# Holding back the output stores of six steps and issuing them from GpSimd in steps 6 and 7 of an mLSTM and mixture-of-depths kernel

## The chip, the core and the metric

The kernel runs on one core of a Trainium2 chip. The core has a matrix engine (TensorE, PE in the profile), a vector engine (DVE), a scalar engine (ACT), GpSimd (POOL) and SyncE (SP), which here only issues DMAs, and 16 DMA engines that all queues share. The engines run side by side and wait for each other through semaphores; each takes its own instructions strictly in order. The metric is the device time of one execution in microseconds, the median of several runs.

## What is computed

The reference has two parts. The first is an mLSTM cell over 4 batches, 8 heads, 768 time steps and a head size of 40, with a matrix state C and a normalizer n for each head:

```python
m_new  = np.maximum(f_gate[:, :, t] + m, i_gate[:, :, t])
f_stab = np.exp(f_gate[:, :, t] + m - m_new)
i_stab = np.exp(i_gate[:, :, t] - m_new)
C = f_stab * C + i_stab * outer(v[t], k[t])
n = f_stab * n + i_stab * k[t]
y[t] = sigmoid(o_gate[t]) * (C @ q[t]) / maximum(abs(n @ q[t]), 1.0)
```

The second is a mixture of depths over the rows x (4 x 768 rows of 320): each batch ranks its rows by a score, and the best 128 go through an MLP and are added back.

```python
scores = x @ w_gate
out = x.copy()
top = argpartition(-scores[b], 128)[:128]
ye  = maximum(x[b, top] @ w1, 0) @ w2
out[b, top] = x[b, top] + sigmoid(scores[b, top]) * ye
```

## The kernel before

The recurrence is worked in blocks of 256 time steps: 3 blocks for each of 4 batches make 12 steps, numbered n = 0 to 11, with batch n // 3. A step is some 8 us long and is a fixed list of work that `_fast` writes out by hand for all engines (the loop of lines 675 to 743); no planner reorders it. For the core of a step TensorE makes `scores(n)`, the transposes of the next step's k and q (`turn`), the state update of the next step (`update`), the reading of the states (`read`), and `attend(n)`; DVE masks, adds up states, and divides (`divide`, which gives y, line 346); ACT copies the transposes out of PSUM and makes the sigmoids.

GpSimd's part matters here. In each step it has `weigh(n + 2)` (line 244: v times the gate columns, two instructions, which wait for the load of v), `output(n)` (line 354: y times the sigmoid gives the rows `x`) and `store(n)` (line 361: two DMAs of 160 KB that write the 256 rows of the step to `out` in DRAM). The rows lie in `x_t`, two buffers that batches use in turn, so steps 0 to 2 write the first, 3 to 5 the second, and 6 to 8 the first again.

Loads of k, v, q, the output gate and the MLP's weights are all issued by SyncE from a queue written by hand (`queue`, line 624), with up to eight in flight; a load waits until its buffer is free, and there are four buffers each for k, v and q.

The second part runs between steps. When a batch's three steps are done its rows are ranked (`ranks`), the 128 chosen row numbers are made (`numbers`, `index`), and GpSimd gathers the chosen rows from `out` in DRAM into `xe` with an indirect DMA (`fetch`, line 523). So a gather reads what the batch's stores wrote. `fetched` then transposes `xe` on TensorE (line 533), `layer1` and `layer2` are the MLP, and `add` scatters its result into `out` with an indirect DMA that adds in DRAM. For batch 0 the row numbers are made in step 4 and fetch(0) is issued in step 6; batch 1 is ranked, gathered and, with batch 0, taken through the MLP in step 8, which has a list of its own (`layers`, lines 628 to 673) that begins, behind the step's scores, with `fetched(0)`. In this list the outputs and stores of steps 6, 7 and 8 stand as well, behind fetch(1). Batches 2 and 3 follow in steps 9 to 11 and at the end.

Some idle places of TensorE hold matmuls that compute nothing (`fill`, line 221).

Of the kernel before, what the change touches and what calls it, by code (L numbers as in the profile page):

```python
# [26 lines left out]
def _fast(ctx, tc, q, k, v, i_gate, f_gate, o_gate, w_gate, w1_in, w2_in, out):  # L27
# [186 lines left out]
    def widen(n):  # L214

        ACT.copy(out=qw_t[n % 2][:, :, :, 0:D], in_=q_t[n % NB].rearrange("s h (t d) -> s t h d", t=2))  # L216
# [30 lines left out]
    def sigmoid(n):  # L247
        for r in range(2):
            for c in range(2):
                ACT.activation(out=so_t[n % 3][64 * c:64 * c + 64, r], in_=o_t[n % NO][64 * r:64 * r + 64, c], func=AF.Sigmoid)  # L250
# [8 lines left out]
    def update(n):  # L259


        spare(n)
        pU = pending[n]["pUt"][:, :, 0:2 * NP * D1].rearrange("e c (p r x) -> e c p r x", r=2, x=D1)
        for c in range(2):
            for p in range(NP):
                for j in range(2):
                    PE.matmul(pU[64 * j:64 * j + 64, c, p], k_t[n % NB][:, c, 2 * p + j, :], wv_t[n % 3][:, c, 2 * p + j],  # L267
                              start=True, stop=True)
        pending[n]["pU"] = pU

    def states(n, i0=0, i1=4):

        for i in range(i0, i1):
            if n % NS == NS - 1 and i == 3:
                return
            C = work.tile([128, NP, D1], FP, name="C", bufs=12)
            src = pending[n]["pU"][:, i // 2, :, i % 2]
            if (n, i) in state:
                DVE.tensor_tensor(out=C, in0=src, in1=state[n, i], op=OP.add)  # L279
                src = C  # L280
            if i < 3:
                if src is not C:
                    DVE.tensor_copy(out=C, in_=src)
                state[n, i + 1] = C
            else:
                b, s = divmod(n + 1, NS)
                DVE.tensor_tensor(out=C, in0=src, op=OP.mult, in1=cols[s][:, 4, b * NP:b * NP + NP].unsqueeze(2)
                                  .to_broadcast([128, NP, D1]))
                state[n + 1, 0] = C

    def scores(n):
        kT, qT = pending[n]["kT"], pending[n]["qT"]
        pS = ps_s.tile([128, 2, 2, NP, 64], FP, name="pS", tag="s")
        for c in range(2):
            for p in range(NP):
                for j in range(2):
                    for r in range(2):
                        e, o = slice(64 * j, 64 * j + D), slice(64 * r, 64 * r + 64)
                        t = slice(128 * c + 64 * r, 128 * c + 64 * r + 64)
                        PE.matmul(pS[o, j, c, p, :], kT[e, p, t], qT[e, p, t], start=True, stop=True)  # L300
        pending[n]["pS"] = pS

    def masked(n):
        P = work.tile([128, 2, 2, NP, 64], FP, name="P")
        flat = "s j c p t -> s (j c p) t"
        DVE.tensor_tensor(out=P.rearrange(flat), in0=pending[n].pop("pS").rearrange(flat), op=OP.mult,  # L306
                          in1=mask.unsqueeze(1).to_broadcast([128, 4 * NP, 64]))
        pending[n]["P"] = P
# [48 lines left out]
    def store(n):  # L357
        b, s = divmod(n, NS)
        for c in range(2):
            a = 256 * s + 128 * c  # L360
            (POOL if n < N - 1 else SP).dma_start(out=out[b, a:a + 128, :].rearrange("(r t) d -> t r d", t=64),  # L361
                          in_=x_t[b % 2][64 * c:64 * c + 64, 2 * s:2 * s + 2, 0:DM])

    def router(n):
        b, s = divmod(n, NS)
        x = x_t[b % 2][:, 2 * s:2 * s + 2]
        scr = work.tile([128, DM], FP, name="scr", bufs=1)
        for r in range(2):
            DVE.tensor_tensor_reduce(out=scr, in0=x[:, r, 0:DM], in1=wg, scale=1.0, scalar=0.0,  # L369
                                     op0=OP.mult, op1=OP.add, accum_out=x[:, r, DM:DM + 1])  # L370
        del pending[n]
# [53 lines left out]
    def ranks(b):  # L425
        x, d = x_t[b % 2], dep[b]
        d["cnt"] = mod.tile([128, 2 * NS], FP, name="cnt")
        for r in range(2 * NS):
            (greater if r < NS else signs)(b, d["sb"], x[:, r, DM:DM + 1], d["cnt"][:, r:r + 1])
        halved(d)  # L430
# [39 lines left out]
    def select(b):  # L470
        sel = mod.tile([128, 2 * NS, 128], BF, name="sel", bufs=1)
        DVE.tensor_tensor(out=sel, in0=iota.unsqueeze(1).to_broadcast([128, 2 * NS, 128]),
                          in1=dep[b]["cnt"].unsqueeze(2).to_broadcast([128, 2 * NS, 128]), op=OP.is_equal)
        dep[b]["sel"] = sel
# [45 lines left out]
    def fetch(b):  # L520

        d = dep[b]
        POOL.indirect_dma_start(out=xe_t[b % 2][:, 0:DM], out_offset=None, in_=out[0:b + 1].rearrange("b s d -> (b s) d"),  # L523
                                in_offset=bass.IndirectOffsetOnAxis(ap=d["idx"], axis=0),
                                bounds_check=(b + 1) * S - 1, oob_is_err=False)
# [102 lines left out]
    def layers(n):  # L628

        fetched(0)  # L630
        read(n)
        ranks(1)
        select(1)
        attend(n)
        layer1(0, 0)
        numbers(1, ps_t.tile([128, 3], FP, name="pi", tag="t"))
        fetch(1)
        sigmoid(n - 2)
        output(n - 2)
        store(n - 2)  # L640
        layer1(0, 4)
        divide(n)
        valued(0)
        sigmoid(n - 1)
        output(n - 1)
        store(n - 1)
        layer2(0)
        router(n - 2)
        router(n - 1)
        fetched(1)  # L650
        weighed(0)
        sigmoid(n)
        output(n)
        store(n)
        valued(1)
        layer1(1, 0)
        router(n)
        layer1(1, 4)
        weigh(n + 1)
        add(0)  # L660
        turn(n + 1, "kT")
        widen(n + 1)
        pB = spread(2, 0, 2 * NS, ps_h, False)
        turn(n + 1, "qT")
        dep[2] = {"sb": spread_copy(pB, 2 * NS)}
        ranks(2)
        layer2(1)
        weighed(1)
        select(2)
        weigh(n + 2)  # L670
        update(n + 1)
        states(n + 1)
        add(1)

    for n in range(N):
        b, s = divmod(n, NS)
        more = n + 1 < N
        todo = queue.get(n, ())
        for act, i in zip(todo[0::2], todo[1::2]):
            act(*(() if i is None else (i,)))  # L680
        scores(n)
        masked(n)
        if n == 8:
            layers(n)
            continue
        if n == 0:
            update(0)
            states(0)
        if n in (3, 6, 11):
            router(n - 1)  # L690
        if n == 4:
            ranks(0)
            select(0)
        if more:
            turn(n + 1, "kT", (0, 2, 6, 2, 2, 4)[n] if n < 6 else 0)
            widen(n + 1)
        if 0 < n and more:
            update(n + 1)
            if n != 9:
                states(n + 1)  # L700
            if n not in (3, 6, 7, 9):
                router(n - 1)
        if not more:
            sigmoid(n)
            gated(n)
            fill(ps_t.tile([128, 128], FP, name="pf", tag="t"), 2)
        read(n)
        if n == 9:
            numbers(2, ps_s.tile([128, 2, 512], FP, name="pi", tag="s")[:, 0, 0:3])
            states(n + 1)  # L710
        if n + 2 < N and n != 7:
            weigh(n + 2)
        if n == 6:
            fetch(0)
        if n == 0:
            update(1)
            states(1)
        if more:
            turn(n + 1, "qT")
            if n in (3, 7):  # L720
                dep[n // 4] = {"sb": spread(n // 4, 0, 2 * NS)}
            if n not in (6, 7):
                sigmoid(n)
        else:
            fetched(b - 1, 2)
            dep[b] = {"sb4": spread(b, 0, 4)}
            layer1(b - 1, 0)
            valued(b - 1)
            ranks_first(b)
        attend(n)  # L730
        divide(n)
        if n == 4:
            numbers(0, spare(n + 1)[:, 1, 0:3])
        if n == 9:
            fetch(2)
        if more and n not in (6, 7):
            output(n)
            store(n)
        if n == 0:
            POOL.memset(k_t[3][:, :, :, D:DP], 0.0)  # L740
            tables()
        if n == 1:
            margins()
# [376 lines left out]
```

## Time and profile before

| | us |
|---|---|
| median of 3 runs | 163.75 (161.92 to 165.38) |
| the profiled execution, its own time | 163.37 |
| its span, first to last instruction | 161.3 |
| granted TensorE clock, mean over the span | 0.989 of full speed |
| GpSimd's DMA queue: bytes, share of the 16 engines' span | 4.92 MB, 11.0% |
| SyncE's DMA queue: bytes, share | 18.75 MB, 65.1% |

The profile is one execution taken by the hardware profiler. A row in order of time gives the start, the busy time, the engine, the line, the operation, output and inputs with their shapes, and how many instructions were merged; the bracket at its end is the idle time of that engine just before, and what released it. A matrix product of float32 appears as two or more instructions. In the rows of DMA issues stand the number of DMAs, the size of each and the median time from the issue to the landing; in those of a queue the packets, the megabytes and the share of all 16 engines in the stretch asked for. A row for a stretch of time gives the busy time of each engine with its count of instructions, then the granted clock, the DMA share (packets in flight overlap, so that it can exceed 1) and GB/s. [...]

### The profile page before, as it was taken

The page shows a single profiled execution, that of the slowest core. Times are in us where ns is not written, and L with a number is a line of the kernel's source. Part 1 is how long each engine was busy: PE and PEld are TensorE (multiplying, and loading weights), DVE is VectorE, ACT ScalarE, POOL GpSimd, SP SyncE. Part 2 cuts the span into 40 slices and gives each one's busy share as a digit, 9 for nine tenths or more (in the row PEclk, how much of TensorE's full clock was granted, in tenths as well). Part 3 has the DMA queues.
Part 4 walks back from the last instruction along what each step waited for, and adds up shares of the span by engine and source line. Part 5 has one row for each costly group of instructions (what it writes and reads, how often), then busy time and mean ns, then how long its engine had stood idle before and what let it go on. Part 6 is the DMA issues. An engine that isn't in the chain of part 4 may idle for free.

```text
span 161.3 us, 6676 instructions
## 1 busy us (share of the span) xinstructions
PE 144.5 (90%) x2864; PEld 125.4 (78%) x2864; DVE 95.2 (59%) x251; ACT 89.0 (55%) x179; POOL 84.5 (52%) x114
## 2 busy tenths in 40 slices
PE   7989899998998998899989989799999999999900
PEld 7779789997987987799878779579888897898500
DVE  6478384656769957594596542197776959411000
ACT  1667396566598747425475675874648669213000
POOL 7137278988575492892004969847480924212020
PEclk9999999999999999999999999999999999999995
DMA  4999899999979989999989999999513210330110
GB/s 88 198 163 196 137 169 205 188 186 205 194 169 227 187 161 208 175 262 296 157 240 232 206 266 172 216 190 184 100 45 87 46 39 4 81 41 0 53 51 2
DMA packets 91880, 24.31 MB, mean 151 GB/s; under 512 B 88097, under 2 KB 90466, under 8 KB 91842
## 3 DMA queue, kind: packets, MB, share of 16 engines
q1 hardware_dynamic: 89920, 18.75, 65.1%
q0 software_dynamic: 1728, 4.92, 11.0%
q8 instruction: 24, 0.39, 1.1%
q10 hardware_dynamic: 194, 0.13, 0.3%
q14 instruction: 14, 0.11, 0.2%
HBM read 19.20 MB, written 4.59 MB: 147 GB/s over the span
## 4 chain that ended last, share of the span: by engine, by line
PE 63%; DMA 14%; ACT 7%; issue 5%; DVE 5%; ACTq 1%; POOL 1%; DVEq 0%; POOLq 0%
PE pt L232 10%; DMA k<-in_k_dram 9%; PE pU L267 9%; PE py L576 8%; PE pH L332 7%; PE pH L322 6%; PE pU L560 6%; PE pS L300 4%; PE ph L560 2%; DMA i_sb<-in_i_gate_dram 2%; PE pU L564 2%; DMA xe<-out_dram,idx 2%; PE pX L498 2%; ACT sgn L423 1%; PE pt L221 1%
## 5 line engine op out<-in xcount | busy, mean ns | idle before, releaser
L244 POOL TENSOR_TENSOR wv<-v,cols 64x656 f32<-64x656 f32 x23 | 30.1, 1312 | 25.0 <-DMA v<-in_v_dram 14.1
L354 POOL TENSOR_TENSOR x<-y,so 128x320 f32<-128x320 f32 x24 | 21.1, 896 | 10.9 <-DVE y L346 4.2
L236 ACT COPY qT<-pt 128x512 f32<-128x512 f32 x24 | 13.8, 635 | 17.2 <-PE pt L232 17.2
L250 ACT ACTIVATE so<-o 64x320 f32<-64x320 f32 x48 | 22.4, 467 | 0.9
L234 ACT COPY kT<-pt 128x512 f32<-128x512 f32 x24 | 13.3, 587 | 15.0 <-PE pt L232 15.0
L369 DVE CUSTOM_DVE_ANT_0 scr<-x,wg 128x320 f32<-128x320 f32 x22 | 13.8, 628 | 8.1 <-POOL x L354 6.5
L576 PE MATMUL py<-w,hT 128*128 128x320 f32 x64 | 18.2, 437 | 0.3 <-ACT qT L236 0.3
L279 DVE TENSOR_TENSOR C<-pU,C 128x164 f32<-128x164 f32 x40 | 13.1, 327 | 7.0 <-PE pU L267 5.9
L267 PE MATMUL pU<-wv,k 128*64 128x82 f32 x384 | 16.5, 237 | 0.7 <-issue 0.7
L267 PEld LDWEIGHTS pU<-wv,k 128*64 128x64 f32 x384 | 14.5, 137 | 2.8 <-issue 2.2
L332 PE MATMUL pH<-wv,P 128*64 128x82 f32 x384 | 16.3, 237 | 0.0
L576 PEld LDWEIGHTS py<-w,hT 128*128 128x128 f32 x64 | 11.8, 190 | 5.1 <-ACT qT L236 0.5
L332 PEld LDWEIGHTS pH<-wv,P 128*64 128x64 f32 x384 | 14.4, 136 | 1.8 <-issue 1.0
L232 PE MATMUL pt<-ident,k 128*128 128x128 f32 x96 | 13.7, 279 | 2.3 <-DMA k<-in_k_dram 2.1
L361 POOL DMA_DIRECT2D out_dram<-x x22 | 13.9, 635 | 3.3 <-POOL x L354 3.3
L418 DVE TENSOR_SCALAR_CACHE_REDUCE cmp<-sb,x 128x768 f32<-128x768 f32 (+2 forms) x14 | 12.0, 857 | 6.0 <-ACT sb L412 5.7
L300 PE MATMUL pS<-qT,kT 40*64 40x64 f32 x768 | 14.8, 221 | 0.8 <-issue 0.5
L306 DVE TENSOR_TENSOR P<-pS,mask 128x1024 f32<-128x1024 f32 x12 | 14.6, 1214 | 0.6 <-PE pS L300 0.6
L523 POOL DMA_INDIRECT xe<-out_dram,idx x4 | 4.3, 1086 | 19.9 <-DVE den L341 13.8
L322 PE MATMUL pH<-C,qT 40*64 40x41 f32 x704 | 14.0, 229 | 0.8 <-issue 0.6
L300 PEld LDWEIGHTS pS<-qT,kT 40*64 40x64 f32 x768 | 12.8, 134 | 2.3 <-issue 0.7
L232 PE MATMUL pt<-ident,qw 128*128 128x128 f32 x96 | 13.1, 279 | 1.4 <-ACT qw L216 1.4
(141 smaller groups left out, 229.6 us busy)
## 6 DMA issues: line engine op xcount, KB each, us to landing
k<-in_k_dram SPq DMA_DIRECT2D x24, 160.0 KB, 5.0
q<-in_q_dram SPq DMA_DIRECT2D x12, 320.0 KB, 5.4
v<-in_v_dram SPq DMA_DIRECT2D x24, 160.0 KB, 4.8
o<-in_o_gate_dram SPq DMA_DIRECT2D x24, 160.0 KB, 5.0
out_dram<-x POOLq DMA_DIRECT2D x22, 160.0 KB, 4.4
w<-in_moe_w_dram SPq DMA_DIRECT2D x2, 640.0 KB, 5.8
w<-in_moe_w_dram SPq DMA_DIRECT2D x2, 512.0 KB, 6.0
out_dram<-x SPq DMA_DIRECT2D x2, 160.0 KB, 2.6
```

Source lines behind the costliest of these rows:

```text
L232: PE.transpose(pt[:, p, :], src[:, c, 2 * p:2 * p + 2, :].rearrange("s j d -> s (j d)"), ident)
L236: ACT.copy(out=T.rearrange("e p (u t) -> e t p u", t=2)[:, c], in_=pt)
L244: (DVE if n == 0 and r else POOL).tensor_tensor(out=wv_t[n % 3][o, :, :, r], in0=v_t[n % NB][o], op=OP.mult, in1=cols[s][o, 0:2, b * H:b * ...
L250: ACT.activation(out=so_t[n % 3][64 * c:64 * c + 64, r], in_=o_t[n % NO][64 * r:64 * r + 64, c], func=AF.Sigmoid)
L267: PE.matmul(pU[64 * j:64 * j + 64, c, p], k_t[n % NB][:, c, 2 * p + j, :], wv_t[n % 3][:, c, 2 * p + j], start=True, stop=True)
L300: PE.matmul(pS[o, j, c, p, :], kT[e, p, t], qT[e, p, t], start=True, stop=True)
L306: DVE.tensor_tensor(out=P.rearrange(flat), in0=pending[n].pop("pS").rearrange(flat), op=OP.mult, in1=mask.unsqueeze(1).to_broadcast([128, ...
L322: PE.matmul(g["pH"][64 * c:64 * c + 64, NP * j + p, r], g["qT"][e, p, t], state[n, 2 * c + r][e, p, :], start=(c, j) not in g["begun"], st ...
L332: PE.matmul(g["pH"][64 * c:64 * c + 64, NP * j + p], g["P"][:, j, c, p, :], wv_t[n % 3][:, c, 2 * p + j], start=(c, j) not in g["begun"], ...
L354: POOL.tensor_tensor(out=x.rearrange(order, j=2, d=D), in0=pending[n]["y"][:, r].rearrange("s (j p) d -> s j p d", j=2), in1=o.rearrange(o ...
L361: (POOL if n < N - 1 else SP).dma_start(out=out[b, a:a + 128, :].rearrange("(r t) d -> t r d", t=64), in_=x_t[b % 2][64 * c:64 * c + 64, 2 ...
L576: PE.matmul(d["py"], hT_t[:, f, half(b)], w2[:, f, :], start=(f == 0), stop=(f == NF - 1))
```

## The change

`store(0)` to `store(5)` no longer stand at the end of their steps. Stores 0 to 2 are issued in step 6, where fetch(0) stood; fetch(0) is moved to the same place of step 7, and stores 3 to 5 follow it there. The stores of steps 6 to 11 stay where they were. All of them but the last are issued by GpSimd, before and after.

```diff
         if n + 2 < N and n != 7:
             weigh(n + 2)
         if n == 6:
+            for i in range(3):
+                store(i)
+        if n == 7:
             fetch(0)
+            for i in range(3, 6):
+                store(i)
         if n == 0:
             update(1)
             states(1)
...
         if more and n not in (6, 7):
             output(n)
-            store(n)
+            if n > 8:
+                store(n)
```

On GpSimd this gives the order: weigh(8), the six DMAs of stores 0 to 2, fetch(0), the six DMAs of stores 3 to 5, fetch(1), output(6). fetch(0) waits for the landing of the first six, fetch(1) for that of all twelve. Between weigh(8) and the first store GpSimd has nothing of step 7 to do, since step 7 has no `weigh` and no `output`. The order of the work on TensorE, DVE, ACT and SyncE is unchanged.

## The prediction

> **What bounds the kernel now.** I read the page first, then TensorE in order of time, then who waited for whom, then GpSimd (POOL) in order of time, and last the DMAs with their time to landing.
>
> ```profile
> PE 144.5 (90%) x2864; PEld 125.4 (78%) x2864; DVE 95.2 (59%) x251; ACT 89.0 (55%) x179; POOL 84.5 (52%) x114
> DMA  4999899999979989999989999999513210330110
> ...
> PE pt L232 <- DMA k<-in_k_dram: 2.1, 5, 0.7
> ...
> 34.64 0.39 PE pt L232 x3
> 35.03 4.65 DMA k<-in_k_dram
> 39.68 0.14 issue
> ```
>
> TensorE is busy for 90% of the span, and the DMA engines are full in nearly every slice up to 28 of 40 (4.03 us each), that is to about 113 us. The waits on loads that reach TensorE are nevertheless short: 2.1 us in five pieces. The chain of waits puts 4.65 us on one load of k, but that is the flight of the DMA, not what TensorE lost. The chain view therefore overstates what faster loads can give; the idle time ahead of TensorE's instructions says it properly:
>
> ```profile
> 39.81 0.63 PE L232 MATMUL pt<-ident,k 128*128 128x128 f32 x4 [0.39 <-DMA k<-in_k_dram]
> 57.47 0.63 PE L232 MATMUL pt<-ident,k 128*128 128x128 f32 x4 [0.27 <-DMA k<-in_k_dram]
> 64.52 0.63 PE L232 MATMUL pt<-ident,k 128*128 128x128 f32 x4 [0.66 <-DMA k<-in_k_dram]
> 65.58 0.63 PE L232 MATMUL pt<-ident,k 128*128 128x128 f32 x4 [0.44 <-DMA k<-in_k_dram]
> ...
> 78.24 1.16 PE L300 MATMUL pS<-qT,kT 40*64 40x64 f32 x64
> 79.34 0.55 PE L533 MATMUL pX<-ident,xe 128*128 128x128 f32 x3
> ```
>
> The four waits in steps 3 to 6 make 0.39 + 0.27 + 0.66 + 0.44 = 1.76 us (the fifth lies at the start, ahead of any store). The last two rows are the place that matters most. At 79.34 step 8 begins its MoE work by transposing `xe`, the rows gathered by fetch(0), right behind the scores and without a wait. When did that gather come in?
>
> ```profile
> 63.45 2.62 POOL L244 TENSOR_TENSOR wv<-v,cols 64x656 f32<-64x656 f32 x2 [2.99 <-DMA v<-in_v_dram]
> 66.15 1.70 POOL L354 TENSOR_TENSOR x<-y,so 128x320 f32<-128x320 f32 x2
> 68.15 1.23 POOL L361 DMA_DIRECT2D out_dram<-x  x2 [0.30 <-POOL x L354]
> 69.39 2.65 POOL L244 TENSOR_TENSOR wv<-v,cols 64x656 f32<-64x656 f32 x2
> 72.33 1.14 POOL L523 DMA_INDIRECT xe<-out_dram,idx  x1 [0.28 <-issue]
> 87.02 1.02 POOL L523 DMA_INDIRECT xe<-out_dram,idx  x1 [13.55 <-DVE den L341]
> ...
> xe<-out_dram,idx POOLq DMA_INDIRECT x1, 6.6
> xe<-out_dram,idx POOLq DMA_INDIRECT x1, 3.4
> ```
>
> The last two rows are the landings of the two gathers, each asked for in a narrow window: fetch(0), issued at 72.33, landed 6.6 us later, at 78.9; fetch(1) needed 3.4. So fetch(0) is hidden with 79.34 - 78.9 = 0.4 us to spare. Whatever is put ahead of it beyond that is paid by TensorE, which takes its instructions in order.
>
> **The change, part by part.** The sum is made against the profiled execution, 163.37 us (a span of 161.3 and 2.1 around it), which lies 0.4 us under the median of 163.75.
>
> *The stores of steps 0 to 5 leave those steps.* Each is two DMAs of 160 KB.
>
> ```profile
> q0 software_dynamic: 124, 0.40, 11.3%
> v<-in_v_dram SPq DMA_DIRECT2D x2, 160.0 KB, 4.6
> 63.17 2.77 SPq L65 DMA_DIRECT2D v<-in_v_dram  x2
> ```
>
> The first row is GpSimd's queue in the window from 36 to 46 us, which holds one pair of stores: 11.3% of 10 us, so 1.1 us of all sixteen engines. Five pairs lie ahead of the load of v for step 8 (issued from 63.17 on, landing 4.6 us later, about 69.2 for the second half), so that load can be up to 5.6 us earlier. The waits on k are 0.27 to 0.66 us long, less than one pair each from step 3 on, so I take all 1.76 us as gone; the bounds are 0 (the queue of loads doesn't speed up) and 1.76 (there is nothing more of this kind to win). What is late next there: nothing but TensorE's own work. GpSimd also loses 12 issues of 0.63 us there, which is worth nothing, as it idles in those steps waiting for v (2.99 us in the row at 63.45).
>
> *Stores 0 to 2 come before fetch(0).* fetch(0) moves behind them, and as it reads the rows that they write it now waits for all six DMAs to land; in the kernel before, its rows had been written long before. The queue up to there:
>
> ```profile
> 63.52 0.82 DVE L346 TENSOR_TENSOR y<-pH,rec 128x640 f32<-128x640 f32 x1
> ...
> L361 POOL DMA_DIRECT2D out_dram<-x x22: 592/628/823, 25.0 to 127.6; - x22
> ```
>
> Step 5's y is ready at 63.52 + 0.82 = 64.34, less the 0.66 us of k waits that lie before it (0.39 + 0.27): 63.7. GpSimd then has output(5), 1.70, and weigh(8), 2.65, which needs v at 65.4: earlier than 69.2 by 3.8 us, with up to 5.6 to be had. It is done at 68.05; with the 0.3 us pause that stands ahead of every first store, six issues of 0.628 us run from 68.35 to 72.1, the last one starting at 71.5. When do they land?
>
> ```profile
> out_dram<-x POOLq DMA_DIRECT2D x2, 160.0 KB, 3.2
> out_dram<-x POOLq DMA_DIRECT2D x2, 160.0 KB, 5.0
> q0 software_dynamic: 1, 0.01, 1.4%
> q0 software_dynamic: 95, 0.32, 22.6%
> 60.00:70.00 10.00, 8.90 (x246) 7.79 (x240) 7.27 (x21) 5.57 (x11) 6.56 (x8) 1.00 0.97 191
> 70.00:80.00 10.00, 9.88 (x307) 8.79 (x301) 5.93 (x15) 4.02 (x8) 3.12 (x3) 1.00 0.98 253
> ```
>
> These are landings of the pairs of step 0 and step 5; then GpSimd's queue between 68.2 and 70.1 us (one packet of step 5's pair) and between 70.1 and 73.7 (the other 95); then the DMA share, 0.97 and 0.98, of the stretches in which the six would run. No trace shows six stores in a row, so I bound them. At best they keep the pace of their issue and the last lands 3.2 us after it starts, at 74.7. At worst each takes what the pair of step 5 took, 3.6 / 2 = 1.8 us, beginning 1.95 us after the first issue: 68.35 + 1.95 + 10.8 = 81.1. Start-up and tail are in those 1.8 us and don't multiply, but the engines are full; I take the middle, 77.9. fetch(0) goes out at 78.0 and its gather needs between 3.4 and 6.6 us, for which I take the mean of the two, 5.0, because loads run beside it as beside both: it lands at **83.0**, with bounds of 78.1 and 87.7.
>
> [...]
>
> *What TensorE makes of it.* It would be ready for `xe` at 79.34 - 1.76 = 77.6 and starts at 83.0 instead: 5.4 us of idle, and 83.0 - 79.34 = 3.7 us later than before. Nothing gives this back: behind it stand step 8's reads, both MoE layers and everything after, and the chain stays on TensorE almost without a break from there to the end. So 163.37 + 3.7 = **167.1**. Queued behind fetch(0) on GpSimd are stores 3 to 5, fetch(1) and the outputs of steps 6 to 8.
>
> *Stores 3 to 5 behind fetch(0).* fetch(0) is issued by 79.1, the six stores by 82.9, and by the same bounds the last lands between 85.5 and 91.9. fetch(1) reads those rows too and waits for them. But it waits for its indices as well, which with a shift of 3.7 come at 87.02 + 3.7 = 90.7, and there is room behind it:
>
> ```profile
> 93.04 0.49 PE L533 MATMUL pX<-ident,xe 128*128 128x128 f32 x3
> ```
>
> 87.02 + 3.4 = 90.4, against a use at 93.04: 2.6 us of cover. The price is nothing until those stores land after 93.3, and one for one from there.
>
> **The rivals.**
>
> *The clock falls in the stall.* No idle of this length stands inside the kernel before, but its end shows one:
>
> ```profile
> 148.33 4.57 PE L576 MATMUL py<-w,hT 128*128 128x320 f32 x16
> 156.00:158.00 2.00, 0.00 (x0) 0.00 (x0) 0.00 (x0) 0.00 (x0) 0.00 (x0) 0.96 0.03 8
> 158.00:160.00 2.00, 0.00 (x0) 0.00 (x0) 0.00 (x0) 0.00 (x0) 0.00 (x0) 0.50 0.00 0
> ...
> 1.12 4.42 PE L99 MATMUL warm<-hot 128*128 128x128 f32 x24 [1.12 <-DVE hot L90]
> 29.80 1.60 PE L221 MATMUL pt<-hot 128*128 128x128 f32 x12
> ```
>
> After the last matmul (148.33 + 4.57 = 152.9) the granted clock is 0.96 over 156 to 158 and 0.50 after: it halved at 157.84, after 4.9 us of idle. My 5.4 us is past that, but by less than the spread of the landing, and it is one event. The price from rows: 24 such matmuls took 4.42 us from a cold start and 12 took 1.60 in mid-kernel, so 4.42 - 3.20 = 1.2 us. Time: 167.1 + 1.2 = 168.3. It decides when the gather lands after 77.6 + 4.9 = 82.5. [...]
>
> *The gather is in time, and the lighter loads win.* If the six stores keep the pace of their issue and the gather is as quick as fetch(1): 74.7 + 3.4 = 78.1. TensorE then starts 1.2 us sooner than before: 162.1. For it speak the 3.2 us of step 0's pair; against it the 5.0 of step 5's and the full engines. It decides at a landing of 79.34. Even with no wait at all the gain ends at 1.76, 161.6.
>
> *The stores start late.* If the load of v for step 8 is not sooner (the queue of loads not helped), weigh(8) starts at 69.4 as before, not at 65.4, everything behind it moves by 4.0 and the gather lands at 87; with the k waits kept and the lower clock that is 163.37 + 7.7 + 1.2 = 172.3; half of that delay gives 170.
>
> That the change does nothing is no rival: GpSimd's order of instructions does have the six stores ahead of each gather.
>
> **How the numbers follow.** Chances: the gather late at full clock 0.40 (its own range 164.5 to 168.5), late with the lower clock 0.30 (167.5 to 170), in time 0.18, stores late or fetch(1) caught 0.12 (169 to 172). A change of 2%, about what a measurement of this kernel tells from none, is 3.3 us: the line is at 167.0. Slower by more: half of 0.40, nearly all of 0.30, most of 0.12, together 0.58. Faster by more would need 160.5, below the 161.6 of the best case: 0.03. The rest, 0.39, within. The range goes from 162.9, inside the early case, to 170.5, inside the late one.
>
> **What would show it.** The k waits of steps 3 to 6 gone from TensorE's rows; six issues in a row on GpSimd at 68 to 69, and fetch(0) not before 75; an idle piece of 3 to 7 us ahead of the first transposes of `xe`, released by the gather; a granted clock of 1.00 behind it, or 0.50 for some microseconds; the landing of six stores between 3.2 and 9.6 us after the last issue. I am wrong if `xe` is there when the scores of step 8 end, if a wait shows up at fetch(1) that TensorE feels, or if the k waits remain.

## The result and the profile after

| | before | after |
|---|---|---|
| median, us | 164.15 (161.92 to 165.38, 4 runs) | 170.72 (170.61 to 170.98, 4 runs) |
| profiled execution, its own time, us | 163.37 | 170.98 |
| its span, us | 161.3 | 169.2 |
| granted TensorE clock, mean | 0.989 | 0.963 |

The changed kernel takes 1.0486 times as long (95% interval 1.0384 to 1.0589). The direction was foreseen; the forecast of 167.1 us was 3.6 us short, and its range ended at 170.5. Ratios here and below are taken on one chip and leave disturbed runs out, which the medians don't; so the two need not agree exactly.

First the page of the changed kernel: busy times, the granted clock in 40 slices (now of 4.23 us each), and one of the costliest groups.

```profile
PE 146.9 (87%) x2864; PEld 128.5 (76%) x2864; DVE 97.7 (58%) x251; ACT 88.7 (52%) x179; POOL 84.2 (50%) x114
...
PEclk9999999999999999999956999999999999999985
...
L369 DVE CUSTOM_DVE_ANT_0 scr<-x,wg 128x320 f32<-128x320 f32 x22 | 17.2, 782 | 6.4 <-POOL x L354 5.0
```

The counts of instructions are those of before (2864, 251, 179, 114), yet TensorE is busy for 146.9 us instead of 144.5. The clock row says why: "56" in the slices from 84.6 to 93.1 us is new. The last row is DVE's product of the rows with the gate weights; its mean, 782 ns, will matter below. The clock row of the kernel before:

```profile
PEclk9999999999999999999999999999999999999995
```

GpSimd in order of time, from step 5's output on:

```profile
65.57 1.69 POOL L354 TENSOR_TENSOR x<-y,so 128x320 f32<-128x320 f32 x2 [2.62 <-DVE y L346]
67.22 3.03 POOL L244 TENSOR_TENSOR wv<-v,cols 64x656 f32<-64x656 f32 x2
70.20 3.79 POOL L361 DMA_DIRECT2D out_dram<-x  x6
80.00 1.12 POOL L523 DMA_INDIRECT xe<-out_dram,idx  x1 [6.01 <-DMA out_dram<-x]
...
95.60 1.07 POOL L523 DMA_INDIRECT xe<-out_dram,idx  x1 [10.93 <-DVE den L341]
```

This is the step that the change was predicted to turn on: six stores in a row, then 6.01 us in which GpSimd waits for their landing, then fetch(0). fetch(1), the last row, was released by DVE and not by a store. On TensorE:

```profile
58.22 1.35 PE L267 MATMUL pU<-wv,k 128*64 128x82 f32 x32 [0.78 <-DVE flags L483]
64.05 1.05 PE L300 MATMUL pS<-qT,kT 40*64 40x64 f32 x57 [0.82 <-issue]
79.04 0.93 PE L332 MATMUL pH<-wv,P 128*64 128x82 f32 x20 [0.69 <-issue]
79.90 1.21 PE L300 MATMUL pS<-qT,kT 40*64 40x64 f32 x64
86.77 0.90 PE L533 MATMUL pX<-ident,xe 128*128 128x128 f32 x3 [5.67 <-DMA xe<-out_dram,idx]
...
89.49 2.40 PE L332 MATMUL pH<-wv,P 128*64 128x82 f32 x32
94.44 0.31 PE L517 MATMUL pi<-place,sel 128*128 128x3 bf16 x6
```

The waits on k have gone from steps 3 to 6, but the scores of step 8 began at 79.90, against 78.24 before: TensorE won nothing there and was 1.66 us later. Besides the pieces shown (0.78, 0.82 and 0.69 us), it lost 0.60 us between the two halves of a transpose, at 73.08. Then it waited 5.67 us for the gather and began `xe` at 86.77, 7.43 us later than before. Behind that, `attend(8)` (line 332) took 2.40 us, and six matmuls of `numbers(1)`, the last row, began at 94.44. The kernel before, in the same view:

```profile
81.94 1.36 PE L332 MATMUL pH<-wv,P 128*64 128x82 f32 x32
...
85.86 0.31 PE L517 MATMUL pi<-place,sel 128*128 128x3 bf16 x6
```

At this row the two are 94.44 - 85.86 = 8.58 us apart: 1.15 more than at `xe`. By the end the spans differ by 169.2 - 161.3 = 7.9, and the times by 7.6. The stretches of 2 us show the reason for the 1.15:

```profile
84.00:86.00 2.00, 0.00 (x0) 0.00 (x0) 1.67 (x4) 0.00 (x0) 0.67 (x2) 0.72 1.07 326
86.00:88.00 2.00, 1.23 (x19) 0.85 (x21) 0.00 (x0) 0.29 (x2) 0.00 (x0) 0.50 1.06 377
88.00:90.00 2.00, 2.00 (x68) 1.92 (x65) 0.00 (x0) 1.92 (x6) 0.00 (x0) 0.50 1.02 240
90.00:92.00 2.00, 2.00 (x31) 1.88 (x28) 0.24 (x2) 1.67 (x4) 0.00 (x0) 0.58 0.59 98
```

TensorE does nothing from 84 to 86, and the DMA engines stay full. The granted clock (third number from the end) falls to 0.72 and then 0.50 inside the wait and stays there while `read(8)` and `attend(8)` run, which is where 2.40 instead of 1.36 us come from.

The chain of waits gives the stretch in which the time was lost:

```profile
73.40 5.69 DMA out_dram<-x
...
79.15 0.85 issue
80.00 6.73 DMA xe<-out_dram,idx
```

The last of the six stores landed at 73.40 + 5.69 = 79.09, and 79.09 - 70.20 = 8.9 us after the first was issued. Then come 0.85 us until the gather is issued and 6.73 until its data are there.

Why did the stores begin at 70.20, when 68.35 was forecast? One reason is that y of step 5 came late. DVE in order of time, after and then before:

```profile
54.76 1.34 DVE L369 CUSTOM_DVE_ANT_0 scr<-x,wg 128x320 f32<-128x320 f32 x1
...
61.70 1.60 DVE L369 CUSTOM_DVE_ANT_0 scr<-x,wg 128x320 f32<-128x320 f32 x1
...
64.57 0.82 DVE L346 TENSOR_TENSOR y<-pH,rec 128x640 f32<-128x640 f32 x1
```

```profile
53.46 0.48 DVE L369 CUSTOM_DVE_ANT_0 scr<-x,wg 128x320 f32<-128x320 f32 x1
```

One such product took 0.48 us before; now one in step 4 took 1.34 and one in step 5 1.60. (Over all 22 the mean of 782 ns stands against 628 before.) GpSimd's rows for the same moments, after and before:

```profile
52.98 2.78 POOL L244 TENSOR_TENSOR wv<-v,cols 64x656 f32<-64x656 f32 x2 [3.97 <-PE pt L232]
...
60.31 2.64 POOL L244 TENSOR_TENSOR wv<-v,cols 64x656 f32<-64x656 f32 x2 [0.88 <-DMA v<-in_v_dram]
```

```profile
54.53 2.63 POOL L244 TENSOR_TENSOR wv<-v,cols 64x656 f32<-64x656 f32 x2 [3.53 <-DMA v<-in_v_dram]
```

With the stores out of the way v comes sooner, and GpSimd now weighs it from 52.98 to 55.76 and from 60.31 to 62.95, just while DVE makes the products. Before, `weigh` was still waiting for v in step 4 (3.53 us) and began as they ended. So the earlier load was paid back on DVE. The product begun at 54.76 ended at 56.10, just behind `weigh` at 55.76, and the one begun at 61.70 ended at 63.30, just behind 62.95.

Against the forecast y is 1.69 us late (65.39, not 63.7). Half of that came by way of TensorE: `attend(5)` ended at 62.96, not 0.66 us ahead of the 62.76 of before, as it stood behind the wait for `flags`, which the products of step 4 had made late. The other half is the products of step 5. The second reason, that v was late too, shows only in two of the experiments (the 28 empty matmuls and the late y).

### The profile page after: what moved, and what is told of

Read it like the earlier page. It is cut to its first block, busy times and chain, and to the rows that moved or that the text cites. A ratio compares the mean times of both kernels' runs of the same rounds, so it can differ in the third digit from the quotient of the medians.

```text
span 169.2 us, 6675 instructions
## 1 busy us (share of the span) xinstructions
PE 146.9 (87%) x2864; PEld 128.5 (76%) x2864; DVE 97.7 (58%) x251; ACT 88.7 (52%) x179; POOL 84.2 (50%) x114
## 4 chain that ended last, share of the span: by engine, by line
PE 64%; DMA 9%; DVE 9%; issue 6%; POOL 4%; ACT 3%; POOLq 0%; DVEq 0%; ACTq 0%
PE pt L232 9%; PE py L576 8%; PE pH L332 7%; PE pU L267 7%; DMA xe<-out_dram,idx 6%; PE pH L322 6%; PE pS L300 6%; PE pU L560 6%; DMA out_dram<-x 3%; PE warm L99 3%; PE ph L560 2%; DVE scr L369 2%; PE pU L564 2%; POOL out_dram L361 2%; DVE cmp L418 2%
## 5 line engine op out<-in xcount | busy, mean ns | idle before, releaser
L244 POOL TENSOR_TENSOR wv<-v,cols 64x656 f32<-64x656 f32 x23 | 30.7, 1336 | 25.8 <-DMA v<-in_v_dram 9.4
L369 DVE CUSTOM_DVE_ANT_0 scr<-x,wg 128x320 f32<-128x320 f32 x22 | 17.2, 782 | 6.4 <-POOL x L354 5.0
L332 PE MATMUL pH<-wv,P 128*64 128x82 f32 x384 | 17.6, 246 | 0.7 <-issue 0.7
L332 PEld LDWEIGHTS pH<-wv,P 128*64 128x64 f32 x384 | 15.5, 144 | 2.7 <-issue 2.1
L300 PEld LDWEIGHTS pS<-qT,kT 40*64 40x64 f32 x768 | 12.8, 134 | 3.4 <-issue 1.9
L322 PE MATMUL pH<-C,qT 40*64 40x41 f32 x704 | 14.8, 236 | 0.3 <-issue 0.3
L322 PEld LDWEIGHTS pH<-C,qT 40*64 40x64 f32 x704 | 13.3, 142 | 2.0 <-issue 1.2
```

What stands on the lines that cost most here:

```text
L244: (DVE if n == 0 and r else POOL).tensor_tensor(out=wv_t[n % 3][o, :, :, r], in0=v_t[n % NB][o], op=OP.mult, in1=cols[s][o, 0:2, b * H:b * ...
L322: PE.matmul(g["pH"][64 * c:64 * c + 64, NP * j + p, r], g["qT"][e, p, t], state[n, 2 * c + r][e, p, :], start=(c, j) not in g["begun"], st ...
L332: PE.matmul(g["pH"][64 * c:64 * c + 64, NP * j + p], g["P"][:, j, c, p, :], wv_t[n % 3][:, c, 2 * p + j], start=(c, j) not in g["begun"], ...
```

## The experiments

Each kernel was run beside the kernel before. Where nothing else is said, the diff is against the changed kernel, and the whole computation is kept.

**Only stores 0 to 2 held.** Does fetch(0) lose its time to the six stores ahead of it, or to the stores behind it?

```diff
             fetch(0)
-            for i in range(3, 6):
-                store(i)
...
-            if n > 8:
+            if n > 2:
                 store(n)
```

> Only stores 0 to 2 are held back and issued in step 6, with fetch(0) behind them in step 7; stores 3 to 5 stay in their steps. Theory (the loss is fetch(0) waiting for six landings, then for packets of the MLP weights that are ahead of it, and the lower clock after the idle): about as slow as the changed kernel, 169 to 172 us, an idle piece of 5 to 7 us ahead of the first transposes of xe, the gather landing 5.5 to 7 us after its issue. Rival (the six stores issued right behind fetch(0) slow the gather, and the late start of the six comes with them): the gather lands in 3 to 4 us, the clock stays at 1.00, 165 to 167 us.

Measured: 173.17 us median, ratio 1.0636 (1.0343 to 1.0929). GpSimd, and TensorE at `xe`:

```profile
80.15 1.11 POOL L523 DMA_INDIRECT xe<-out_dram,idx  x1 [6.46 <-issue]
...
86.64 0.90 PE L533 MATMUL pX<-ident,xe 128*128 128x128 f32 x3 [7.64 <-DMA xe<-out_dram,idx]
```

The gather still takes 86.64 - 80.15 = 6.5 us with no store issued behind it. Stores 0 to 2 alone do the whole damage; stores 3 to 5 don't slow the gather. That it came out slower than expected is in part the clock: TensorE waited 7.64 us, the clock stayed low until about 93.7, and `numbers(1)` began 8.63 us behind `xe` (95.27), against 7.67 in the changed kernel. That is 1.0 of the 2.2 us between the two spans (171.4 and 169.2); the rest lies further behind and stays open.

**Only stores 3 to 5 held,** fetch(0) back in step 6:

```diff
         if n == 6:
-            for i in range(3):
-                store(i)
-        if n == 7:
             fetch(0)
+        if n == 7:
...
-            if n > 8:
+            if n < 3 or n > 8:
                 store(n)
```

> Only stores 3 to 5 are held back and issued in step 7; stores 0 to 2 stay in their steps and fetch(0) in step 6. Theory: no six landings ahead of fetch(0), so no idle piece over 1 us at xe and the time within 1% of the kernel before, 163 to 165.5 us; fetch(1) is not delayed by the six stores. Rival (the burst of stores is itself the cost, through the DMA engines and fetch(1)): 166.5 us or more, with the second gather waiting for the stores.

Measured: 164.50 us, ratio 1.0142 (0.9931 to 1.0354).

```profile
79.72 0.55 PE L533 MATMUL pX<-ident,xe 128*128 128x128 f32 x3
...
82.57 0.88 PE L322 MATMUL pH<-C,qT 40*64 40x41 f32 x23 [1.36 <-issue]
```

No wait at `xe`, and no loss that can be told from none, though the interval is wide. That stores 3 to 5 stand late has no price that shows, as predicted.

**Twenty empty matmuls ahead of the transposes,** to keep the clock up during the wait:

```diff
-        fetched(0)
+        fetched(0, 20)
```

> The changed kernel with 20 matmuls that compute nothing on TensorE ahead of the transposes of xe, some 5.1 us by the 1.60 us that 6 of them take elsewhere, so that TensorE has nearly no idle there. Theory (the granted clock of 0.50 for 6.8 us is a part of the loss of its own): granted clock 1.00 throughout, the reads and attends of step 8 back to 3.2 us together from 4.3, the time 1 to 2 us under the changed kernel, 168.7 to 169.7 us. Rival (the lower clock costs nothing, as the work behind it waits for other things): no change, 170.5 to 171 us.

Measured: 170.50 us, ratio 1.0503 (1.0233 to 1.0774): a miss. TensorE, and the stretches behind:

```profile
79.31 4.73 PE L221 MATMUL pX<-hot 128*128 128x128 f32 x40
...
85.65 0.55 PE L533 MATMUL pX<-ident,xe 128*128 128x128 f32 x3 [1.61 <-DMA xe<-out_dram,idx]
```

```profile
86.00:88.00 2.00, 2.00 (x84) 1.82 (x84) 0.00 (x0) 1.71 (x5) 0.00 (x0) 0.91 1.09 387
88.00:90.00 2.00, 2.00 (x23) 1.82 (x20) 0.00 (x0) 1.94 (x5) 0.00 (x0) 0.50 1.06 237
```

The empty work ended 1.61 us too soon, and the clock went to 0.50 all the same, about 2 us after work had resumed. So this run says nothing about the price.

**Twenty-eight of them,** so that no gap is left (same line, 28 for 20):

> The changed kernel with 28 empty matmuls ahead of the transposes of xe in place of 20, some 6.6 us by what the 20 took (4.73), so that no idle over 1 us is left there. Theory (the lower clock is a cost of its own, and the 1.6 us of idle that 20 matmuls left were enough for it): granted clock 1.00 up to the end, reads and attends of step 8 at 1.14 and 1.36 us, 168.3 to 169.7 us. Rival (the clock falls for another reason, or its loss is made up for): the clock falls again, or the time stays at 170.2 to 171.

Measured: 169.27 us, ratio 1.0331 (1.0209 to 1.0454).

```profile
86.67 0.49 PE L533 MATMUL pX<-ident,xe 128*128 128x128 f32 x3
...
88.16 1.36 PE L332 MATMUL pH<-wv,P 128*64 128x82 f32 x32
...
92.43 0.30 PE L517 MATMUL pi<-place,sel 128*128 128x3 bf16 x6 [0.28 <-DVE sel L472]
```

`xe` is begun at the same moment as in the changed kernel (86.67 against 86.77), the clock never falls in mid-kernel, `attend(8)` is back at 1.36 us, and `numbers(1)` begins 92.43 - 86.67 = 5.76 us behind `xe` instead of 94.44 - 86.77 = 7.67. The lower clock costs 1.9 us here; the profiled executions differ by 170.98 - 169.13 = 1.85. (The price rests on these rows: the intervals of the two ratios overlap.)

Up to step 8 GpSimd's list is that of the changed kernel, and y of step 5 came 0.58 us sooner in this execution (64.81). The stores nevertheless began at 70.13 against 70.20, because `weigh(8)` waited for v:

```profile
67.32 2.87 POOL L244 TENSOR_TENSOR wv<-v,cols 64x656 f32<-64x656 f32 x2 [0.63 <-DMA v<-in_v_dram]
```

**The weights w2 loaded later.** Between 80 and 85 us of the changed kernel GpSimd's queue, in which the gather lies, moved next to nothing:

```profile
q1 hardware_dynamic: 1856, 1.41, 97.7%
q0 software_dynamic: 7, 0.03, 2.0%
...
xe<-out_dram,idx POOLq DMA_INDIRECT x1, 6.7
```

SyncE's queue (q1) was moving mostly w2, two loads of 640 KB. Put behind the load of v for step 9 (`load_v` loads v alone, `load_kq` k and q):

```diff
-... 5: (load_o, 7, weights2, None, load_o, 8), 6: (load, 9),
+... 5: (load_o, 7, load_o, 8), 6: (load_v, 9, weights2, None, load_kq, 9),
```

> The changed kernel with the second MLP weight loaded later by four DMAs (behind the gate of step 8 and v of step 9, ahead of k and q of step 9), so that its large packets no longer fly when fetch(0) is issued. Theory (GpSimd's queue gets no turn while the weights' packets fill the engines): the gather lands 3 to 4.5 us after its issue in place of 6.7, the idle is under 4.9 us so that the clock stays, 165.5 to 168 us. Rival (the gather is slow because twelve stores surround it): it lands in 6 to 7 us again, 170 to 171.5 us.

Measured: 169.58 us, ratio 1.0495 (1.0360 to 1.0631).

```profile
79.46 1.11 POOL L523 DMA_INDIRECT xe<-out_dram,idx  x1 [5.73 <-DMA out_dram<-x]
...
83.83 0.90 PE L533 MATMUL pX<-ident,xe 128*128 128x128 f32 x3 [4.37 <-DMA xe<-out_dram,idx]
```

The gather now takes 83.83 - 79.46 = 4.4 us: that part of the theory holds. `xe` begins 2.94 us sooner than in the changed kernel, but the profiled execution is only 1.95 us shorter (169.03 against 170.98), the median 1.1, and the ratio, taken on another chip, no better than the changed kernel's. A wait of 4.37 us still brings the clock down, to 0.50 from 84 to 88 us, and `numbers(1)` begins 7.92 us behind `xe` (91.75), against 5.76 at full clock.

**Both together,** w2 later and 19 empty matmuls:

> The changed kernel with the second weight loaded later and with 19 empty matmuls ahead of the transposes of xe, some 4.5 us. Theory (the parts add up: the gather's wait behind the weights' packets, some 2 us, and the clock, some 2 us): gather landing 4 to 5 us after its issue, granted clock 1.00 up to the end, 166.8 to 168.3 us. Rival (the two are one loss counted twice): no better than either part alone, 169 to 170 us.

Measured: 166.80 us, ratio 1.0144 (1.0090 to 1.0198).

```profile
84.68 0.55 PE L533 MATMUL pX<-ident,xe 128*128 128x128 f32 x3 [0.98 <-DMA xe<-out_dram,idx]
...
90.49 0.30 PE L517 MATMUL pi<-place,sel 128*128 128x3 bf16 x6 [0.28 <-DVE sel L472]
```

The clock does not fall, and `numbers(1)` begins at 90.49 instead of 94.44. By these rows the slow gather and the clock together are worth 3.95 us, and by the medians 3.9; the two ratios would make it 1.0486 - 1.0144, about 3.4% or 5.6 us of 164, but they come from different chips. What is left, 90.49 - 85.86 = 4.6 us at this row against the kernel before, is the landing of the stores with the gather behind it.

**The late y.** Is it the router's products on DVE, run beside `weigh`? The products of step 5's list moved behind `divide(5)`:

```diff
-            if n not in (3, 6, 7, 9):
+            if n not in (3, 5, 6, 7, 9):
                 router(n - 1)
...
         divide(n)
+        if n == 5:
+            router(n - 1)
```

> The changed kernel with the router of step 4 (two DVE products of 0.48 us each, when nothing disturbs them) moved behind the division of step 5. Theory (the six stores started 1.85 us later than forecast because the lighter loads let weigh(7) on GpSimd run while DVE does these products, which then take 1.1 us more and delay step 5's y): y ready 0.8 to 1.3 us sooner against the end of attend(5), the six stores from 68.8 to 69.5 us in place of 70.2, the gather up to 1.2 us sooner, 169 to 170.6 us. Rival (the late start came from TensorE alone): the stores start at 70.0 to 70.4 again and the time stays at 170.5 to 171.

Measured: 172.57 us, ratio 1.0517 (1.0465 to 1.0569). y of step 5 ended at 64.08 instead of 65.39 us; 0.45 of that is a lead that this execution already had when `attend(5)` ended (62.51 against 62.96), and 0.86 is the products. But GpSimd's next link then waits for v, and stores and gather come as late as ever:

```profile
66.99 2.79 POOL L244 TENSOR_TENSOR wv<-v,cols 64x656 f32<-64x656 f32 x2 [0.70 <-DMA v<-in_v_dram]
...
86.21 0.90 PE L533 MATMUL pX<-ident,xe 128*128 128x128 f32 x3 [6.97 <-DMA xe<-out_dram,idx]
```

That the products delay y is shown. That the late y delays the stores is not: they began 0.48 us sooner (69.72 instead of 70.20), about the lead of the execution, and `xe` 0.56, because v was there only at 66.99. The clock was low from 81 to 91 us here; `numbers(1)` still began 0.51 us sooner (93.93). That the time is no better comes from behind 115 us, in part from a piece of 0.41 put down to TensorE's issue.

**Held, but let out in time.** Stores 0 to 2 in step 4, fetch(0) in step 6, stores 3 to 5 in step 7. If holding itself costs or wins something, it must show here:

```diff
-        if n == 6:
+        if n == 4:
             for i in range(3):
                 store(i)
-        if n == 7:
+        if n == 6:
             fetch(0)
+        if n == 7:
```

> All six stores are held back as in the changed kernel, but stores 0 to 2 come out two steps sooner, in step 4, fetch(0) stands in step 6 as in the kernel before, and stores 3 to 5 come out in step 7. Theory (the price is the nearness of the six stores to fetch(0)): the six land long before fetch(0) is issued, which goes out at 70 to 72 us, no idle piece over 1.5 us at xe, 162.5 to 165.5 us. Rival (holding stores back and letting six out at once is what costs, through the loads of k and v that they hold up): waits on k of over 2 us in steps 4 to 6, 167 us or more.

Measured: 164.22 us (10 runs), ratio 1.0012 (0.9958 to 1.0067): no change. Who TensorE waited for:

```profile
PE pS L300 <- issue: 1.7, 3, 0.8
...
PE pU L267 <- DVE flags L483: 1.2, 1, 1.2
...
PE pt L232 <- DMA k<-in_k_dram: 0.4, 1, 0.4
```

The waits on k, 2.1 us in five pieces before, are down to one of 0.4. In their place stand a wait for DVE's `flags` (1.2 us; before, they were ready in time) and pieces put down to TensorE's own issue. Relief of the loads is real, and no gain shows.

**The same with the row numbers and products moved on DVE,** to take the new wait away as well (the diff is against the kernel just above):

```diff
-            if n not in (3, 6, 7, 9):
+            if n not in (3, 4, 5, 6, 7, 9):
                 router(n - 1)
...
         attend(n)
-        divide(n)
         if n == 4:
             numbers(0, spare(n + 1)[:, 1, 0:3])
+        divide(n)
+        if n in (4, 5):
+            router(n - 1)
```

> The kernel with stores 0 to 2 let out in step 4 and 3 to 5 in step 7, in which moreover the routers of steps 3 and 4 stand behind the divisions of steps 4 and 5, and batch 0's row numbers are made ahead of the division of step 4. Theory (what the waits on k hid was DVE's chain to the row numbers, made longer by GpSimd's products beside it): the 1.2 us that TensorE waits for the row numbers ahead of update(6) goes, waits on k stay away, 161.5 to 163.5 us, 0.5 to 1.5% under the kernel before. Rival (the lighter loads have nothing to give whatever stands in the way): as without the reordering, 163 to 165 us.

Measured: 165.94 us (12 runs), ratio 0.9982 (0.9928 to 1.0035). The wait for `flags` is gone, and the gain isn't there either. In the profiled execution TensorE lost 1.91 us in one piece instead, and then the clock:

```profile
81.72 0.88 PE L322 MATMUL pH<-C,qT 40*64 40x41 f32 x23 [1.91 <-issue]
```

**That reordering alone,** in the kernel before, nothing held:

> The kernel before with the same reordering of DVE's work in steps 4 and 5, and no store held back. Theory: the waits on k (1.4 us in steps 4 to 6) stay as they are and hide the reordered work, so that the time is that of the kernel before within 0.5%. Rival (the reordering is worth something by itself): 0.5% or more faster than the kernel before.

Measured: 163.42 us (12 runs), ratio 0.9892 (0.9851 to 0.9933). This beats the kernel before by its interval, by 1.1%. The four waits on k are still there (2.0 us), so it has nothing to do with the stores. The kernel just above differs from it by the held stores alone and was run on the same chip: 0.9982 against 0.9892, with intervals that just meet. So beside this reordering, holding the stores looks like a loss of 0.9% and not like a gain. Its profiled execution, 165.0 us, was above its median and doesn't show where the 1% comes from; that stays open.

**Two that tried to give fetch(0) more room.** In the first, the kernel before issues it a step earlier, in step 5 ahead of `weigh(7)`, to test whether its 0.4 us of margin makes the spread of its times:

> The kernel before with fetch(0) one step sooner, in step 5 ahead of weigh(7), and nothing held back. Theory (in the kernel before the gather landed with 0.4 us to spare, so it is late in some executions and not in others): issued near 61 us, landed by 68, the time 161 to 163.5 us with little spread. Rival (the gather's landing is nowhere near deciding in the kernel before): the same times and the same spread as the kernel before.

Measured: 166.80 us (163.06 to 168.82, 4 runs), against 162.22 to 172.79 for the kernel before on that chip; no interval could be made. The second half of `weigh(7)` came late, behind the gather (at 66.46, after GpSimd had idled for 3.09 us), and TensorE waited 2.0 us for it. The spread remained. Inconclusive.

In the second, the same move stands in the kernel that holds only stores 3 to 5:

> Stores 3 to 5 held back to step 7, stores 0 to 2 in their steps, and fetch(0) in step 5 ahead of weigh(7). Theory: with the gather out of the way the lighter loads of steps 4 to 6 show, up to the 1.4 us of waits on k of those steps, 160 to 162.5 us. Rival (what those waits hid is next late, DVE and instruction issue, so that nothing is won): no faster than the kernel with fetch(0) in step 5 alone, 161.5 to 164 us.

Measured: 164.59 us (10 runs), ratio 1.0046 (0.9988 to 1.0104): nothing won.

## Why the prediction fell short, point by point

**The mechanism** was right. fetch(0), put behind six stores that it must see landed, becomes the wait that ends last; TensorE idled 5.67 us at `xe`, and 5.4 were forecast. That this is nearly equal is luck, and hides two errors of the same size: TensorE was ready for `xe` at 79.90 + 1.21 = 81.1, not 77.6, and the gather was there at 86.7, not 83.0.

**The step that failed** is the sum at the gather's landing, 83.0 us. It was 3.77 us short. Its four terms:
- "it is done at 68.05", for `weigh(8)`, and the first store at 68.35: it was 70.20, 1.85 late. Two conditions failed, and either was nearly enough. First, `weigh(8)` "needs v at 65.4", and v was there at 66.99 and 67.32 in the two kernels with the same stores whose rows show the wait; its load was issued only 3.06 us sooner than before (60.11 against 63.17). Second, y of step 5 ended at 65.39, not 63.7, because the earlier loads moved GpSimd's `weigh` onto DVE's products; the prediction took the earlier load as a gain without asking what the engine that it releases would collide with. The kernel with the products moved mends the second and starts the stores hardly sooner, as the first remains. `weigh(8)` itself took 3.03, not 2.65, and the 0.3 us pause ahead of the first store did not come. In the prediction's own terms this is its rival "The stores start late", at somewhat less than half of its 4.0 us; for half it had named 170.
- The drain of the six stores was nearly right: 8.9 us from first issue to last landing, 9.55 taken, from bounds of 6.3 to 12.8.
- From that landing to the gather's issue 0.9 us passed, 0.1 taken.
- "the mean of the two, 5.0": the gather took 6.77. Both prices stood in the profile of before, and the mean was taken because "loads run beside it as beside both". They weren't the same loads: the gather of 6.6 us flew beside weights, the one of 3.4 didn't. The kernel with w2 moved shows it: 4.4 us.

**"What is late next there: nothing but TensorE's own work"** failed. The waits on k did go, but `flags`, 0.78, issue pieces of 0.82 and 0.69, and 0.60 inside a transpose took their place. Two kernels that keep most of this relief (waits on k of 0.4 and 0.8 us) without the late gather, with stores 0 to 2 let out in step 4, gained nothing: 1.0012 and 0.9982.

**The lower clock** was named as a rival with 0.30 and priced at 1.2 us. It happened, as in each of the four profiled executions with a wait of over 4 us at `xe` (4.37, 5.67, 6.97 and 7.64). The 4.9 us of idle that the prediction took as its condition are no threshold: the clock fell some 3.1, 3.8, 1.8 and 4.4 us into these waits. (In the changed kernel a mean of 0.72 from 84 to 86 us is 1.1 us at half clock, so it fell at 84.9, 3.8 us behind the 81.1 at which the wait began; the others are worked out in the same way.) Its price is 1.9 us. The warm-up matmuls from which 1.2 was taken stand at a granted clock of 1.00 from 0 to 6 us, so they priced a slow start and no stretch of low clock that could be counted; here the clock was low for 6.8 us, and TensorE worked in 4.9 of them.

**Stores 3 to 5 behind fetch(0) cost nothing,** and fetch(1) was not caught: both as forecast; it was released by DVE. **Behind `xe`** "nothing gives this back" held but for 0.7 us.

Together: 3.7 foreseen, 3.77 more at the gather, 1.15 for the clock net of gaps that the kernel before had there, less 0.7 given back by the end of the span and 0.3 around it, make 7.6.

## What to carry to other kernels

A gather that reads stores back from DRAM is tied to their landing, so price the whole chain (the engine that makes the rows, the issues, the drain, the gather) and ask of each link what flies beside it; a landing time needn't hold beside other traffic (the gather took 6.77 us beside w2 and 4.4 without it). A load that comes sooner also makes its consumer start sooner (`weigh` at 52.98 instead of 54.53), and a GpSimd operation that moves onto a DVE product can cost more than the wait that went (here 0.86 us of y against 0.66 of waits on k). If a wait of several microseconds on TensorE can't be avoided, count the clock behind it (1.9 us here).

## What the runs showed of the hardware

**The clock.** The low stretches in mid-kernel counted here lasted 3.4, 6.8 or 10.2 us, one, two or three times the shortest. The kernel that held only stores 3 to 5:

```profile
82.00:84.00 2.00, 1.43 (x33) 1.35 (x35) 1.93 (x5) 1.94 (x5) 0.00 (x0) 0.63 0.95 314
84.00:86.00 2.00, 2.00 (x29) 1.82 (x26) 1.47 (x4) 0.28 (x2) 0.00 (x0) 0.52 1.09 357
```

A stretch of 2 us at a mean of c has stood 2 x (1 - c) / 0.5 us at half clock, so these two make 4 x (0.37 + 0.48) = 3.4 us. The changed kernel's four stretches from 84 to 92 us make 4 x (0.28 + 0.50 + 0.50 + 0.42) = 6.8, twice that; with only stores 0 to 2 held, and with the products moved, it was 10.2. The clock fell at an idle piece of 1.36 us in the kernel that held only stores 3 to 5, at one of 1.61 behind the twenty empty matmuls, and at one of 1.09 in the kernel with the stores let out in step 4. It did not at 1.36 in the kernel that only issues fetch(0) in step 5, nor at 1.16 in the last kernel above: `attend(8)` behind took 1.36 us in both, as in the kernel before at a granted clock of 1.00. So it isn't the length of the piece alone that decides.

**Two queues.** Beside w2 the gather's queue moved 7 packets in 5 us and the other 1856; none of the 7 fell between 80 and 84 us, though the gather had been issued at 80.00. With w2 moved its queue had 164 packets from 79 to 85 us, beside 4222 of the other, the gather having been issued at 79.46. Why the gather's queue moved so little beside w2 isn't settled.

**TensorE's issue pieces.** In front of the second part of `read(8)`, 23 matmuls, stood a piece of 0.61 us before and of up to 1.91 in other kernels. The DMA queues show one packet of 16 KB of instructions shortly ahead. From 80.0 to 80.5 us in the kernel with only stores 3 to 5 held, whose piece ended at 82.57:

```profile
q8 instruction: 1, 0.02, 11.0%
```

In the kernel before it begins between 78.5 and 79.0, and the piece ends at 81.45; with the stores let out in step 4, between 79.5 and 80.0, and 82.36; in the reordered version of that, between 79.0 and 79.5, and 81.72. So the piece ends 2 to 3 us behind the start of the packet each time. In the changed kernel the packet begins between 80.0 and 80.5, while TensorE was about to wait for `xe`, and there is no piece. Whether the piece waits for the packet isn't shown, as no run delayed or hastened one.
